# Third and later batches loaded in six pieces instead of four, and 50 dummy matmuls of two widths instead of 30 of one

## The chip, the cores and the metric

One NeuronCore of one Trainium2 chip runs the whole program, attention and expert layer, as one launch. The metric is the device time of one execution in microseconds (us).

## What is computed

Eight batches of eight heads attend over 576 positions of 64 dimensions, each query to itself and the 63 positions before it. The result is laid out as 4608 tokens of 512 numbers. A gate gives each token a score for each of eight experts; all scores are taken in descending order, and a token goes to the expert of its best score that still has room (576 tokens each). Each expert is two matrix products with a ReLU between them.

```python
scores = scale * np.matmul(q, k.transpose(0, 1, 3, 2))
mask = (rel >= 0) & (rel < 64)          # rel = pos_q - pos_k
attn = softmax(np.where(mask, scores, -1e9))
x = (attn @ v)                          # -> (4608, 512)
logits = x @ w_gate                     # -> (4608, 8)
for idx in np.argsort(-logits.flatten()):   # greedy, cap 576 tokens an expert
    ...
out[mask_e] = np.maximum(x[mask_e] @ w1[e], 0.0) @ w2[e]
```

## The kernel before

The program has two stages, one after the other. The first is attention, some 150 us; the second takes the experts one after another.

Attention works on blocks of 64 positions, nine in a batch, and on two blocks at once: iteration `m` of the loop in `attention` (`M` is 36) takes blocks 2m and 2m+1 of the 72. `qk` (L128) multiplies queries by the keys of the block and the one before; VectorE adds the mask and takes the row's extreme (L136); ScalarE takes the exponential (L141); `tr` turns the result on TensorE (L148), ScalarE copies it out (L153); `pv` (L178), two iterations later, multiplies by V; `norm` divides on VectorE (L218, tile `x`) and hands `x` to a list of stores. Once for each batch, `gate_mm` (L85) multiplies a transposed copy of V (tile `VT`) by the gate's weights, `gate_cp`, `gate_tr` and `gate_out` (L89, L95, L101) put the result into spare columns of the V tile `VO`, and GpSimd makes a shifted copy `VE` (L114, L115). For batches 3 to 7 both halves of `gate_mm` stand in the batch's first iteration: eight matmuls for blocks 0 to 3, eight for blocks 4 to 8.

All loads and the stores of `x` are issued by SyncE in the order in which they are written. Batches 0 and 1 are loaded in slices written out by hand (L235 to L253). From the third batch on `load_all` (L255) loads `Q` and `K` (part 0) and, an iteration later, `VT` and `VO` (part 1); each of the four tensors goes in four DMAs (L267), 288 KB or 292 KB each, 2304 or 2336 bytes in each of 128 partitions, and what is left of `VO` in a fifth (L269). In DRAM `lay` has put the data of one DMA together. Stores are held back: `HOLD` is 14, and tile `x` has `HOLD + 4` = 18 buffers, so the `x` of iteration j+18 is written into the buffer that the store of j has read.

Each DMA that SyncE issues takes one of eight completion semaphores in turn, and waits until the DMA that had that semaphore before has landed.

Before anything has arrived, TensorE runs `WARM` dummy matmuls of 128 columns on a tile of zeros (L48, L49); their result is never read.

Of the kernel before, what the change touches and what calls it, by code (L numbers as in the profile page):

```python
# [20 lines left out]
B, H, S, D = 8, 8, 576, 64  # L21
NB = S // 64
HP = H // 2
E = 8
WARM = 30
VW = 73
DM = H * D
HOLD = 14
LOADED = 9 * (B - 3) + 12


def attention(ctx, tc, c, q, k, v, vt, gate, xs, L, choices, setup, counters, mean, rows, guess):

    nc = tc.nc
    wgbd, wg = gate
# [6 lines left out]
    x = ps.tile([128, 512], FT, name="Tp", bufs=2)  # L42
    SP = [ps.tile([128, 2, 4, 128], FT, name=f"Sp{r}", bufs=1) for r in range(2)]

    z = c["zero"]
    nc.vector.memset(z, 0.0)

    for _ in range(WARM):  # L48
        nc.tensor.matmul(x[:, 0:128], z, z, start=True, stop=True)  # L49
    masks(tc, c)  # L50
    Q, K, VO, VE, VT = {}, {}, {}, {}, {}

# [202 lines left out]
    def load_all(b, part):  # L255
        if not part:
            Q[b] = ld.tile([128, NB, HP, 64], FT, name="Q", bufs=3)
            K[b] = ld.tile([128, NB, HP, 64], FT, name="K", bufs=3)
        else:
            VT[b] = ld.tile([128, NB, HP, 64], FT, name="VT")  # L260
            VO[b] = ld.tile([128, 5, H, VW], FT, name="VO", bufs=3)
        for t, x in ((VT[b], vt), (VO[b][:, 0:4], v)) if part else ((Q[b], q), (K[b], k)):
            t = t.rearrange("p i h w -> p (i h w)").rearrange("p (n x) -> p n x", n=4)
            n = 512 * t.shape[2]
            rows = x[b].rearrange("p x -> (p x)")[0:n].rearrange("(n p x) -> n p x", n=4, p=128)
            for i in range(4):
                nc.sync.dma_start(t[:, i], rows[i])  # L267
        if part:
            nc.sync.dma_start(VO[b][0:64, 4].rearrange("p h w -> p (h w)"),  # L269
                              v[b].rearrange("p x -> (p x)")[n:n + 64 * H * VW].rearrange("(p x) -> p x", p=64))  # L270
# [13 lines left out]
    def store(m, x):  # L284
        nc.sync.dma_start(xs[128 * m:128 * m + 128], x.rearrange("p h d -> p (h d)"))
# [5 lines left out]
    for m in range(M + 1):  # L291
# [62 lines left out]
        for s in (2 * m, 2 * m + 1):  # L354
            if stores and (len(stores) > HOLD or s > LOADED):
                store(*stores.pop(0))
        for x in loads.get(m, []):
            load_all(*x)
# [26 lines left out]
def masks(tc, c):  # L385

    nc, cp = tc.nc, c["pool"]
    jp, rel = c["jp"], c["rel"]
    nc.vector.tensor_copy(rel[0:64], jp[0:64])
    nc.vector.tensor_scalar(rel[64:128], jp[64:128], 64, None, op0=OP.add)  # L390
    far = cp.tile([128, 128], FT, name="far")
    near = cp.tile([128, 128], FT, name="near")
    c["mask"] = {}

    def make(kinds):
        m = c["mask"][kinds] = cp.tile([128, 128], FT, name=f"mask{kinds[0]}{kinds[1]}")
        for a, kind in enumerate(kinds):
            r = slice(64 * a, 64 * a + 64)
            if kind:
                nc.vector.tensor_tensor(m[r], far[r], near[r], OP.add)  # L400
            else:
                nc.vector.tensor_scalar(m[r], rel[r], 0.0, -8.0e9, op0=OP.is_gt, op1=OP.mult)

    nc.vector.tensor_scalar(far, rel, 0.0, -8.0e9, op0=OP.is_le, op1=OP.mult)
    nc.vector.tensor_scalar(near, rel, 64.0, -8.0e9, op0=OP.is_gt, op1=OP.mult)
    make((0, 1))
    make((1, 1))
    c["ident"] = cp.tile([128, 128], FT, name="ident")
    c["identr"] = cp.tile([128, 128], FR, name="identr")
    nc.vector.tensor_scalar(c["identr"], jp, 0.0, None, op0=OP.is_equal)  # L410
    nc.vector.tensor_scalar(c["ident"], jp, 0.0, None, op0=OP.is_equal)
    make((1, 0))


def lay(q, k, v, wg):
    import numpy as np
    def blocks(t):
        t = t.reshape(B, HP, 2, NB, 64, D).transpose(0, 2, 5, 3, 1, 4)
        return np.ascontiguousarray(t).reshape(B, 128, NB * HP * 64)

    va = np.zeros((B, 640, H, VW), np.float32)
    va[:, :S, :, :D] = v.transpose(0, 2, 1, 3)
    va[:, :S, :, VW - 1] = 1.0
    va = np.ascontiguousarray(va.reshape(B, 5, 128, H * VW).transpose(0, 2, 1, 3)).reshape(B, 128, 5 * H * VW)

    def pieces(t, n):

        t[2:] = t[2:].reshape(B - 2, 128, n, -1).transpose(0, 2, 1, 3).reshape(B - 2, 128, -1)
        return t

    wb = np.zeros((128, HP, 32), np.float32)
    w = wg.reshape(HP, 2, D, E)
    wb[0:64, :, 0:8] = w[:, 0].transpose(1, 0, 2)
    wb[64:128, :, 16:24] = w[:, 1].transpose(1, 0, 2)
    return dict(q=pieces(blocks(q), 4), k=pieces(blocks(k), 4), v=pieces(va, 5), vt=pieces(blocks(v), 4), wg=wb)


NT = 4608
# [976 lines left out]
def body(tc, q, k, v, vt, wg, w1, w2, xs, out):  # L1415
    nc = tc.nc
    with ExitStack() as ctx:
# [6 lines left out]
        with ExitStack() as actx:  # L1424
            attention(actx, tc, c, q, k, v, vt, (wgs, wg), xs, L, lambda j0, j1: rt.choices(j0, j1, 0), rt.setup,
                      rt.counters, (rt.mean, rt.mean_mm, rt.mean_out), rt.rows, rt.guess)
# [49 lines left out]
```

## Time and profile before

| what | us |
|---|---|
| median of 3 runs (lowest, highest) | 612.87 (612.52, 614.18) |
| the profiled execution: its own time | 613.34 |
| its span, first to last instruction | 611.7 |
| PE busy in the span (5713 matmuls, with as many weight loads) | 588.9 |
| ACT busy | 371.8 |
| DVE busy | 394.1 |

The span lies 1.64 us below the profiled execution's own time. In the profile PE is the matmul unit of TensorE and PEld its weight loads, DVE is VectorE, ACT ScalarE, POOL GpSimd and SP SyncE; L12 is line 12 of the kernel, and `out<-in` names tiles. "issue" as the reason of a wait means that nothing in the profile ended it. Queue q1 holds the DMAs that SyncE issues; the queue of kind "instruction" with the number q8 moves packets of 16 KB.

### The profile page before, as it was taken

The numbers are of one execution on the slowest core, as the hardware profiler recorded it, in microseconds if no ns is written. First come the engines' busy times: TensorE is split into PE (matmuls) and PEld (weight loads), VectorE is DVE, ScalarE is ACT, GpSimd is POOL, SyncE is SP. The second block draws the span as 40 slices with busy tenths as digits, with TensorE's granted clock in tenths as the row PEclk, the third lists the DMA queues.
The fourth block names the chain that finished last, engine by engine and source line by source line (L and its number), as shares of the span: only waits on it lengthen the run. The fifth ranks groups of instructions, "written<-read, shape, count | busy, mean of one in ns | idle before, by whom it ended". The sixth has DMA issues, their size and how long they took to land.

```text
span 611.7 us, 15537 instructions
## 1 busy us (share of the span) xinstructions
PE 588.9 (96%) x5713; PEld 503.3 (82%) x5713; DVE 394.1 (64%) x1804; ACT 371.8 (61%) x804; POOL 198.4 (32%) x277
## 2 busy tenths in 40 slices
PE   7899999997699999999999999999999999999995
PEld 6677878886499789878988997898899789889984
DVE  6798988888785587369547936773685466705400
ACT  6799989997465477267537735852774375615410
POOL 1334435862431261054117203511530273011011
PEclk9999999998699999999999999999999999999999
DMA  8999999962698699189748938992895689410001
GB/s 314 362 359 358 362 365 376 384 240 89 183 242 173 247 210 243 43 289 229 152 167 229 245 70 270 216 221 97 257 243 111 233 191 330 169 44 34 2 26 53
DMA packets 46104, 128.87 MB, mean 211 GB/s; under 512 B 5824, under 2 KB 6464, under 8 KB 46016
## 3 DMA queue, kind: packets, MB, share of 16 engines
q1 hardware_dynamic: 31744, 79.00, 36.0%
q0 software_dynamic: 13984, 48.25, 34.1%
q8 instruction: 46, 0.75, 0.5%
q10 hardware_dynamic: 288, 0.52, 0.3%
q14 instruction: 42, 0.34, 0.2%
HBM read 82.14 MB, written 18.87 MB: 165 GB/s over the span
## 4 chain that ended last, share of the span: by engine, by line
PE 50%; issue 15%; DMA 5%; POOL 2%; DVE 1%; ACT 1%; POOLq 0%; SPq 0%
PE h L1328 23%; PE o L1372 20%; PE o L1362 4%; DMA st<-w 2%; DMA wl<-st 2%; POOL out L1351 2%; PE tp L1266 1%; DMA xg<-xs,idx 1%; PE rps L685 1%; PE rps L1046 1%; POOL xg L1228 0%; ACT wh L1155 0%; POOLq L1472 0%; POOL wl L1171 0%; DVE hl L1297 0%
## 5 line engine op out<-in xcount | busy, mean ns | idle before, releaser
L1328 PE MATMUL h<-xh,wh 128*128 128x320 f32 (+2 forms) x800 | 159.0, 333 | 0.3 <-DVE hh L1297 0.3
L1328 PEld LDWEIGHTS h<-xh,wh 128*128 128x128 f32 x800 | 124.2, 188 | 5.6 <-ACT sum L1287 0.5
L1351 POOL DMA_INDIRECT out<-ot,idx x40 | 40.1, 1001 | 198.1 <-DVE q L932 82.1
L1372 PE MATMUL o<-wh,hl 128*128 128x512 f32 x256 | 101.3, 396 | 0.0
L1372 PE MATMUL o<-wl,hh 128*128 128x512 f32 x256 | 100.5, 393 | 0.0
L1372 PE MATMUL o<-wh,hh 128*128 128x512 f32 x256 | 100.4, 392 | 0.0
L141 ACT ACTIVATE pe<-st,mx 128x128 f32<-128x128 f32 x288 | 92.0, 394 | 5.4 <-DVE mx L136 5.0
L1328 PE MATMUL h<-xh,wl 128*128 128x256 f32 (+1 forms) x512 | 91.1, 298 | 0.0
L1328 PEld LDWEIGHTS h<-xh,wl 128*128 128x128 f32 x512 | 78.5, 188 | 4.1
L1171 POOL DMA_DIRECT2D wl<-st x51 | 45.9, 1023 | 82.1 <-ACT wl L1169 43.8
L1155 ACT ACTIVATE wh<-st 128x1024 fp32r<-128x1024 f32 x64 | 67.3, 1051 | 4.9 <-DMA st<-w 4.7
L1342 ACT ACTIVATE ot<-o 128x512 f32<-128x512 f32 x32 | 19.2, 599 | 83.7 <-PE o L1372 83.7
L136 DVE CUSTOM_DVE_ANT_0 st<-Sp,mask 128x128 f32<-128x128 f32 x288 | 63.7, 285 | 5.9 <-PE Sp L128 4.5
L1372 PEld LDWEIGHTS o<-wl,hh 128*128 128x128 f32 x256 | 48.1, 188 | 9.5
L1372 PEld LDWEIGHTS o<-wh,hh 128*128 128x128 f32 x256 | 48.1, 188 | 9.4
L1372 PEld LDWEIGHTS o<-wh,hl 128*128 128x128 f32 x256 | 48.1, 188 | 9.3
L1169 ACT ACTIVATE wl<-wh 128x1024 fp32r<-128x1024 f32 x51 | 53.9, 1058 | 1.0
L1289 DVE TENSOR_TENSOR sum<-h,sum 128x256 f32<-128x256 f32 x56 | 23.4, 418 | 40.3 <-ACT sum L1287 39.7
L1292 ACT ACTIVATE hh<-h 128x320 fp32r<-128x320 f32 (+1 forms) x72 | 30.8, 427 | 30.2 <-PE h L1328 30.0
L1228 POOL DMA_INDIRECT xg<-xs,idx x32 | 32.4, 1012 | 42.2 <-DVE eq L970 34.6
L1297 DVE SCALAR_TENSOR_TENSOR hl<-h,hh 128x256 fp32r<-128x256 f32 x72 | 30.0, 417 | 24.1 <-ACT hh L1292 24.0
L153 ACT ACTIVATE pt<-Tp 128x512 f32<-128x512 f32 x70 | 41.1, 587 | 6.7 <-PE Tp L148 6.6
(222 smaller groups left out, 1028.4 us busy)
## 6 DMA issues: line engine op xcount, KB each, us to landing
st<-w SPq DMA_DIRECT2D x59, 512.0 KB, 7.6
wl<-st POOLq DMA_DIRECT2D x51, 512.0 KB, 8.6
xs<-x SPq DMA_DIRECT2D x36, 256.0 KB, 5.8
VO<-v SPq DMA_DIRECT2D x24, 292.0 KB, 6.4
Q<-q SPq DMA_DIRECT2D x24, 288.0 KB, 6.9
K<-k SPq DMA_DIRECT2D x24, 288.0 KB, 6.2
VT<-vt SPq DMA_DIRECT2D x24, 288.0 KB, 5.8
st<-w POOLq DMA_DIRECT2D x5, 512.0 KB, 7.9
```

The costliest lines, as they stand in the source:

```text
L136: nc.vector.tensor_tensor_reduce(st[:, h, :], Sp[h % 2][:, h // 2], mk, scale=-0.125, scalar=3.0e38, op0=OP.add, op1=OP.min, accum_out=mx[ ...
L141: nc.scalar.activation(pe[:, h, :], st[:, h, :], AF.Exp, bias=mx[:, h:h + 1], scale=-1.0)
L153: return pt, lambda: nc.scalar.activation(flat, Tp, AF.Copy)
L1155: nc.scalar.activation(hi, st[i], AF.Copy)
L1169: nc.scalar.activation(lo, hi.bitcast(FT), AF.Copy, scale=-1.0)
L1171: nc.gpsimd.dma_start(lo.bitcast(FT), st[i], accum_op=OP.add)
L1228: nc.gpsimd.indirect_dma_start(out=g[a][0:n], out_offset=None, in_=self.xs, in_offset=IndirectOffsetOnAxis(ap=idx[0:n, a:a + 1], axis=0))
L1292: nc.scalar.activation(hh[:, f, c0:c1], h, AF.Relu)
L1297: nc.vector.scalar_tensor_tensor(t, h[:, a - c0:b - c0], 0.0, hh[:, f, a:b].bitcast(FT), op0=OP.max, op1=OP.subtract)
L1328: nc.tensor.matmul(h[:, 0:w], wv[:, cc, 128 * (f % 2):128 * (f % 2) + 128], x[:, cc, x0:x0 + w], start=(k == 0), stop=(k == 4 * len(terms) ...
L1351: nc.gpsimd.indirect_dma_start(out=self.out[5 * p + a], out_offset=IndirectOffsetOnAxis(ap=idx[0:m, a:a + 1], axis=0), in_=ot[0:m], in_off ...
L1372: nc.tensor.matmul(o, ht[:, f, 128 * a:128 * a + 128], wt[:, 512 * (f % 2):512 * (f % 2) + 512], start=(k == 0), stop=(k == 23))
```

## The change

In `load_all` each of the four tensors of a batch from the third on goes in six DMAs of 192 KB (1536 bytes in a partition; for `VO` 1536 or 1664 bytes) in place of four; `pieces` computes the cuts, and `lay` puts the data in DRAM in the new order. The remainder of `VO` and the first two batches are as they were. The 30 dummy matmuls of 128 columns become 32 of 16 columns and then 18 of 128, all with the same 128x128 weights of zeros.

```diff
-WARM = 30
+WARM, SHORT = 18, 32
+def pieces(n):
+    cuts = [n * i // (6 * 32) * 32 for i in range(7)]
+    return list(zip(cuts, cuts[1:]))

-    for _ in range(WARM):
-        nc.tensor.matmul(x[:, 0:128], z, z, start=True, stop=True)
+    for n in [16] * SHORT + [128] * WARM:
+        nc.tensor.matmul(x[:, 0:n], z, z[:, 0:n], start=True, stop=True)

-            t = t.rearrange("p i h w -> p (i h w)").rearrange("p (n x) -> p n x", n=4)
-            n = 512 * t.shape[2]
-            rows = x[b].rearrange("p x -> (p x)")[0:n].rearrange("(n p x) -> n p x", n=4, p=128)
-            for i in range(4):
-                nc.sync.dma_start(t[:, i], rows[i])
+            t = t.rearrange("p i h w -> p (i h w)")
+            rows = x[b].rearrange("p x -> (p x)")
+            n = 128 * t.shape[1]
+            for i, j in pieces(t.shape[1]):
+                nc.sync.dma_start(t[:, i:j], rows[128 * i:128 * j].rearrange("(p x) -> p x", p=128))
```

## Rows read from the trace of the kernel before

**Rows 1.** Busy us by stretch: PE, PEld, DVE, ACT, POOL; clock, DMA share, GB/s.

```profile
20.00:131.00 111.00, 108.71 (x2220) 87.27 (x2217) 97.79 (x679) 102.81 (x307) 56.39 (x105) 1.00 1.03 368
131.00:150.00 19.00, 16.52 (x365) 14.45 (x362) 16.70 (x101) 17.56 (x62) 9.10 (x16) 1.00 0.21 81
```

**Rows 2.** Waits of the weight loads, 0 to 150: total us, times, longest.

```profile
PEld Op L178 <- issue: 5.4, 14, 1.5
...
PEld Tp L85 <- issue: 2.5, 4, 2.0
```

**Rows 3.** Waits of SyncE, 0 to 160: total us, times, longest.

```profile
SPq L267 <- DMA VO<-v: 15.1, 25, 1.8
```

**Rows 4.** Timeline of PE, 14.9 to 22: start, us, what, [idle before].

```profile
15.09 1.10 PE L128 MATMUL Sp<-K,Q 64*64 64x128 f32 x32
...
18.24 0.73 PE L85 MATMUL Tp<-VT,wgs 128*32 128x320 f32 x5 [1.39 <-issue]
...
21.79 0.45 PE L128 MATMUL Sp<-K,Q 64*64 64x128 f32 x8
```

**Rows 5.** Timeline of PEld, 86.3 to 90.

```profile
88.87 0.13 PEld L178 LDWEIGHTS Op<-VE,pt 128*64 128x64 f32 x1 [1.47 <-issue]
```

**Rows 6.** Timeline of all engines, 44 to 66: three successive iterations.

```profile
44.00 1.10 PE L128 MATMUL Sp<-K,Q 64*64 64x128 f32 x32
...
48.20 1.10 PE L128 MATMUL Sp<-K,Q 64*64 64x128 f32 x32
...
51.49 1.10 PE L128 MATMUL Sp<-K,Q 64*64 64x128 f32 x32
```

**Rows 7.** DMA queues: packets, MB, share; the whole span, then 18.24 to 88.87.

```profile
q8 instruction: 46, 0.75, 0.5%
...
q8 instruction: 11, 0.18, 1.1%
```

**Rows 8.** Timeline of SyncE: issues of DMAs, x how many in the row.

```profile
17.33 0.43 SPq L67 DMA_DIRECT2D Q<-q  x1
17.81 0.43 SPq L67 DMA_DIRECT2D K<-k  x1
...
22.67 3.05 SPq L267 DMA_DIRECT2D Q<-q  x4
...
46.14 2.59 SPq L267 DMA_DIRECT2D VT<-vt  x4
...
98.28 2.55 SPq L285 DMA_DIRECT2D xs<-x  x4
```

**Rows 9.** DMA queue q1, 124 to 128 (2048-byte packets), then 25.1 to 28.

```profile
q1 hardware_dynamic: 877, 1.60, 105.0%
...
q1 hardware_dynamic: 292, 1.20, 102.1%
```

**Rows 10.** Issue to landing: VT issued at 48.3, xs at 98.28, xs after 130.

```profile
DMA to landing us min/median/max: 7.4/7.4/7.4
...
DMA to landing us min/median/max: 6.3/6.3/6.3
...
DMA to landing us min/median/max: 2.0/2.0/2.1
```

**Rows 11.** Timeline: gate_mm of batch 3, and the write of x(24).

```profile
57.11 1.18 PE L85 MATMUL Tp<-VT,wgs 128*32 128x256 f32 x16
...
109.14 0.68 DVE L218 TENSOR_TENSOR x<-Op,r 128x512 f32<-128x512 f32 x1
```

**Rows 12.** Lines L49 and L1048: ns min/median/max, first and last start us.

```profile
L49 PE MATMUL Tp<-zero x30: 288/314/315, 1.1 to 4.2; 128*128 128x128 bf16 x30
...
L1048 PE MATMUL rps<-B,R x18: 247/248/270, 158.2 to 159.2; 128*72 128x64 bf16 x18
```

**Rows 13.** Line L128, semaphore instructions of its queue, in the same columns.

```profile
L128 PEldq EVENT_SEMAPHORE  x18: 51/51/51, 4.9 to 123.0; - x18
```

More of the change, by code (lines that the diff above doesn't have):

```diff
@@ L424, in lay, with apart @@
     va = np.ascontiguousarray(va.reshape(B, 5, 128, H * VW).transpose(0, 2, 1, 3)).reshape(B, 128, 5 * H * VW)
-    def pieces(t, n):
-        t[2:] = t[2:].reshape(B - 2, 128, n, -1).transpose(0, 2, 1, 3).reshape(B - 2, 128, -1)
+    def apart(t, n):
+        cuts = pieces(n) + [(n, t.shape[2])] * (n < t.shape[2])
+        t[2:] = np.concatenate([t[2:, :, i:j].reshape(B - 2, -1) for i, j in cuts], 1).reshape(B - 2, 128, -1)
         return t
@@ L434, in lay @@
     wb[64:128, :, 16:24] = w[:, 1].transpose(1, 0, 2)
-    return dict(q=pieces(blocks(q), 4), k=pieces(blocks(k), 4), v=pieces(va, 5), vt=pieces(blocks(v), 4), wg=wb)
+    n = NB * HP * 64
+    return dict(q=apart(blocks(q), n), k=apart(blocks(k), n), v=apart(va, 4 * H * VW), vt=apart(blocks(v), n), wg=wb)
 NT = 4608
```

## The prediction

> **What bounds the kernel now.** I first read the busy time by stretch, because the change touches only the attention stage. From 20 to 131 us PE, ACT and DVE are busy 98, 93 and 88% of the time and the DMA engines 103% by the profile's account, at 368 GB/s [rows 1]. After 131 the DMA share is 0.21 with the compute engines as busy as before [rows 1]: the loads are done some 19 us before attention is. So the DMA queue is full, but it runs ahead of the work, and what sets the end of attention is the chain PE, DVE, ACT, with an iteration of 3.29 us (48.20 to 51.49) and 4.20 us where a half `gate_mm` is added (44.00 to 48.20) [rows 6]. Whatever attention gains or loses goes to the end: the expert stage starts from its last result.
>
> Next I looked in the waits of TensorE's queue for time that this chain doesn't explain. No wait for a load stands among the large ones. Two are put down to "issue", which is nothing that the profile knows: 2.0 us in `gate_mm` and 1.5 us in `pv` [rows 2]. The timeline places them. The iteration that starts at 15.09 ends at 21.79, 6.70 us in place of 4.20, with PE stopped until 18.24 in the middle of eight matmuls on one load, of which three had run; the other stop ends at 88.87, after 1.47 us [rows 4, 5]. I read both as **instruction fetches that come late**. Queue q8 moves 46 packets of 16 KB in the run, against 11,426 matmuls and weight loads, about one for 250 of them, and between the ends of the two stops lie exactly 11 such packets [rows 7]. TensorE's stream is thus read in blocks of some 250 instructions, through the DMA engines that the loads fill, and a block that is still behind loads stops TensorE.
>
> The loads in front of it are many: a load from the third batch on takes 6 to 7 us to land where the engines are busy [rows 10], and SyncE spends its time waiting for the eighth DMA back [rows 3]. At 288 KB that is 2.36 MB in flight.
>
> **Loads in six pieces.** Eight in flight become 1.57 MB, two thirds. What a fetch has to wait behind shrinks in that proportion if it waits behind all of it. The stop at 88.87 lasted 1.47 us, and the other 13 "issue" waits at that line are 0.30 us each ((5.4 - 1.5) / 13) [rows 2], so **1.2 us** are to be had. The bounds are 0 (the fetch waits for something else) and 1.5. I take 1.2, since a third off a wait of several us is more than the stop.
>
> The price is in the packets. Between 124 and 128 us they are of 2048 bytes, with one of 4 bytes for every eight: 877 x 8/9 = 780 took 4 x 16 x 1.050 = 67.2 us, 86.2 ns each. From 25.1 to 28 the mean is 1.20 MB / 260 = 4620 bytes, and 2.9 x 16 x 1.021 / 260 = 182.2 ns [rows 9]. The slope is 0.0373 ns a byte, so a packet of 1536 bytes should take 67.1 ns and one of 2304 95.8; three of the first against two of the second are 201.3 against 191.6, **5.1% more**. From below the price is 0 (the bytes are the same). I take 5.1%, because 2048 is near. Loads from the third batch on begin at 22.67 [rows 8].
>
> [...]
>
> Is there cover for it? I looked for the first places where loads are nearly late. (1) The second eight `gate_mm` of batch 3 start half way through 57.11 to 58.29, at about 57.6 [rows 11]; the last quarter of `VT` that they read, the fourth issue of the row at 46.14, went out at 48.3 and landed 7.4 us later, at 55.7 [rows 8, 10]. Slack 1.9; loss until then (48.3 - 22.7) x 5.1% = 1.3; **left 0.6**. (2) The write of x(24) at 109.14 needs the store of x(6), issued at 98.28 and landed 6.3 later, at 104.6 [rows 8, 10, 11]. Slack 4.5; this store stands behind five whole batches, so the loss is at most (98.28 - 22.67) x 5.1% = 3.9, less for the stores among them, say 3.4; **left 1.1**. Against the times of before nothing is late, but what is left is also the most that compute can run ahead of its old times: 0.6 at batch 3, 1.1 at x(24). At the end the loads finish 4 us later and the last 25 stores, queued behind them on SyncE, catch up 4 us later, inside the stretch that has a DMA share of 0.21: cost 0.
>
> SyncE issues eight DMAs more a batch. Unhindered it issues one in 0.48 us (17.33 to 17.81) [rows 8]; a piece will take the engines 8 x 67.1 = 537 ns. It keeps up, narrowly. Eight pieces in flight are 4.3 us of work, and a store issued alone lands in 2.0 [rows 10], so the engines don't run dry. Each piece is one landing more to wait for: 48 in all. The nearest row is a semaphore instruction of TensorE's queue, 51 ns [rows 13]: 48 x 51 = 2.4 us from above if all are on PE's path, 0 if they pass while TensorE waits for DVE or ACT anyway. I take 0, since the waits of this kind are there now, 18 of them, without an iteration that shows it.
>
> **The dummy matmuls.** 30 start between 1.1 and 4.2, 107 ns apart [rows 12], which is 128 columns at 1.2 GHz, the lower level. Eighteen of them are 1.9 us. For the 32 short ones no row is of that size. With 18 matmuls of 64 columns at the lower level, 60 ns apart (158.2 to 159.2) [rows 12], 32 take 1.9 us from above; from below 16/128 of 107 ns, 0.4 us. Together 2.3 to 3.8 in place of 3.2; the first real matmul waits for its load until 4.9 anyway [rows 13], and 1.1 + 3.8 = 4.9 just reaches it. Cost 0. If weight loads hold them to 107 ns they end at 6.5 and the first matmul comes 1.6 us late. If TensorE came to its upper level later after them, an iteration before 16 us would lose about the 1.10 us that its first 32 matmuls take [rows 4], ahead of a stop that hides it if it stays. What they do beside that: 20 matmuls with their weight loads are **40 instructions more** ahead of everything, so every block of the stream ends 40 instructions earlier in the work. The block whose end stopped PE at 18.24 would end in the matmuls that start at 15.09 [rows 4], and its fetch be asked for about 1 us earlier, behind less. That stop may shrink from 2.0 us to nothing, or stay and only sit elsewhere; the early loads are unchanged. Bounds 0 and 2.0; I take 1.0, of which the 0.6 of place (1) can pass.
>
> [...]
>
> **The sum.** 0.6 at the start and 1.2 at 88 make 1.8, and place (2) lets 1.1 through. From the profiled execution's 613.34: 612.2. It lies 0.47 above the median of 612.87, so against the median 611.8.
>
> **The rivals.** *First case, the forecast*: 611.8, between 611.0 and 612.5. Chance 0.42. *Second, the fetch is late for another reason, or the stops move*: TensorE's blocks end elsewhere and one of the next ends stops it as long. For it: both stops come when a block's crossing and the queue meet by chance, and of the blocks between them none stopped PE long; against it: less is in flight. No gain, 612.9, between 612.5 and 613.7. Chance 0.30. *Third, the pieces cost nothing* (bytes set the rate, the bound of 0): then, if both stops go, place (1) lets 1.9 through and place (2) 4.5, and the gain is 1.9 + 1.2 = 3.1: 609.8. [...] Chance 0.16. *Fourth, SyncE or the packets become the bound and attention waits for loads*: it decides where a DMA takes over 0.55 us, since then the loss at x(24), five batches of 24, passes the 1.1 left. An issue takes 0.48 unhindered and (3.05 - 0.43) / 3 = 0.87 in the row at 22.67, waits for landings included [rows 8]; I price the case a quarter of the way, at 0.58. A batch then takes 24 x (0.58 - 0.537) = 1.0 longer than in the forecast, and x(24) comes 5 x 1.0 - 1.1 = 3.9 late: 612.87 + 3.9 = 616.8. For it: the margin of 0.48 against 0.54 is thin; against it: 0.48 was reached with the queue full. Late dummies or 2.4 us of semaphores would end near it, at 614.5 to 615.3. Chance 0.12.
>
> **How the numbers follow.** About 0.3%, 1.8 us, is what a measurement of this kernel can tell from no change: below 611.0 is faster, above 614.7 slower. The third case (0.16) and a quarter of the first, where the packets cost half of what I take (0.10), make 0.26 faster; the fourth, without its mildest part, makes 0.10 slower; 0.64 lies within. The range goes from the third case's 609.8 to 614.2, which leaves most of the fourth and the tail of the third outside, some 2 in 10.
>
> **What would show it.** Right: the wait of 1.47 us before `pv` is gone and no other "issue" wait over 1 us stands after 23 us; the stop near 16 us is shorter; DMA rates of 350 to 365 GB/s from 23 to 115; x(24) is written right after the store of x(6) lands. Wrong: PE waiting for `VT`, `K` or `VO` (fourth case), the first real matmul after 5.0 (dummies), a DMA rate as before (third), or stops of the same length at other lines (second).

## The result and the profile after

The changed kernel takes 620.17 us (median of five runs, 619.59 to 622.30) against 612.87 us: **slower by 7.3 us**, ratio 1.0123 with a 95% interval of 1.0098 to 1.0148. The profiled execution took 621.69, its span is 620.0. The forecast was 611.8, at most 614.2; what came lies beyond even the fourth case.

The loss is all in attention. Its last `qk` starts at 148.2 in the profiled execution and at 139.4 in that of before, 8.8 us later; from there to the end both take the same within 0.5 us. The rows, of the kernel before and of the changed one:

```profile
139.43 1.10 PE L128 MATMUL Sp<-K,Q 64*64 64x128 f32 x32
```

```profile
148.25 1.10 PE L134 MATMUL Sp<-K,Q 64*64 64x128 f32 x32
```

The same stretches as [rows 1], busy us by engine, clock, DMA share and GB/s:

```profile
20.00:131.00 111.00, 101.85 (x2032) 82.05 (x2031) 88.94 (x616) 92.86 (x275) 51.13 (x93) 0.97 0.97 318
131.00:150.00 19.00, 19.00 (x407) 15.60 (x405) 17.39 (x120) 18.07 (x55) 13.07 (x27) 1.00 0.93 344
```

The loads now come at 318 GB/s in place of 368, and they go on behind 131 us, where the DMA share was 0.21 and is 0.93. The share between 20 and 131 has hardly fallen (1.03 to 0.97), so the share alone would not have told. The time of a packet counts in full, however slow it is: from 23 to 115 us the changed kernel's packets of 1536 bytes take 65 ns in the median, 75.7 in the mean and up to 1.7 us. The rate tells.

The waits up to 150 us (total, times, longest) name the places:

```profile
PEld Op L184 <- issue: 4.6, 14, 0.7
...
PEld Tp L91 <- issue: 3.9, 3, 3.4
...
DVE x L224 <- DMA xs<-x: 3.4, 1, 3.4
PE Tp L91 <- DMA VT<-vt: 3.0, 1, 3.0
...
DVE VO L107 <- DMA VO<-v: 1.7, 1, 1.7
```

L184 is `pv`: its longest "issue" wait is 0.7 us where [rows 2] had 1.5. L91 is `gate_mm`: its "issue" wait of 3.4 us is no late fetch but the weight load beside the 3.0 us in which TensorE waits for `VT`. The timeline of TensorE shows both sides of the trade, the stop of [rows 4] gone and the iteration of place (1) drawn out:

```profile
15.38 1.10 PE L134 MATMUL Sp<-K,Q 64*64 64x128 f32 x32
...
19.98 0.83 PE L134 MATMUL Sp<-K,Q 64*64 64x128 f32 x16
...
56.05 1.10 PE L134 MATMUL Sp<-K,Q 64*64 64x128 f32 x32
57.97 0.64 PE L91 MATMUL Tp<-VT,wgs 128*32 128x256 f32 x8 [0.81 <-ACT pe L147]
61.58 0.92 PE L91 MATMUL Tp<-VT,wgs 128*32 128x320 f32 x8 [2.97 <-DMA VT<-vt]
...
65.99 0.56 PE L134 MATMUL Sp<-K,Q 64*64 64x128 f32 x12
```

The iteration at 15.38 takes 4.60 us, 2.1 less than in [rows 4]. The one at 56.05 takes 9.94, where the same one of before takes 4.34:

```profile
56.08 1.10 PE L128 MATMUL Sp<-K,Q 64*64 64x128 f32 x32
...
60.42 1.10 PE L128 MATMUL Sp<-K,Q 64*64 64x128 f32 x32
```

The waits of 0.81 and 2.97 us are 3.8 of the 5.6 us that it lost. Most of the rest is a second price of the stop. After it the granted clock of TensorE (the third number from the right) is below 1.00:

```profile
61.58:66.00 4.42, 4.42 (x49) 3.41 (x50) 1.25 (x6) 1.29 (x4) 0.46 (x1) 0.61 0.86 259
```

The mean of 0.61 is 3.4 us, from 62.0 to 65.4, at 0.50, the lower of the two levels, 1.00 and 0.50, that its records show. From the second eight `gate_mm` to the next `qk` it now takes 4.41 us, where before it took some 2.8 (57.6, half way through that row of [rows 11], to 60.42). The clock falls to 0.50 a second time, from 120.0 to 123.5, behind the stop at place (2). In the kernel before it stays at 1.00 between 20 and 131 us. Place (2) shows in VectorE's timeline (compare [rows 11]):

```profile
117.80 0.69 DVE L224 TENSOR_TENSOR x<-Op,r 128x512 f32<-128x512 f32 x1 [3.37 <-DMA xs<-x]
```

Two more views tell how the loads are fed. SyncE's waits up to 160 us, the first line of them beside [rows 3]:

```profile
SPq L273 <- DMA VO<-v: 5.0, 9, 1.6
SPq L273 <- DMA K<-k: 5.0, 10, 1.1
SPq L273 <- DMA VT<-vt: 4.4, 11, 2.2
SPq L273 <- DMA Q<-q: 3.7, 9, 1.6
```

By these lines SyncE waited 39 times for a landing for 144 loads, 18.1 us in all; the first line of before alone has 25 waits and 15.1 us for 96 loads. So SyncE was more often behind the engines than before. Even so, counted from issue to landing over 23 to 115 us, 7.6 DMAs were in flight on average, and 7.95 before: most of the time there were nearly eight. Part 6 of the page gives KB and median us from issue to landing, first of the kernel before, then of the changed one:

```profile
VO<-v SPq DMA_DIRECT2D x24, 292.0 KB, 6.4
Q<-q SPq DMA_DIRECT2D x24, 288.0 KB, 6.9
K<-k SPq DMA_DIRECT2D x24, 288.0 KB, 6.2
VT<-vt SPq DMA_DIRECT2D x24, 288.0 KB, 5.8
```

```profile
Q<-q SPq DMA_DIRECT2D x36, 192.0 KB, 4.4
K<-k SPq DMA_DIRECT2D x36, 192.0 KB, 4.5
VT<-vt SPq DMA_DIRECT2D x36, 192.0 KB, 5.3
VO<-v SPq DMA_DIRECT2D x30, 192.0 KB, 4.8
```

A piece is two thirds of the old size but takes 0.64 to 0.91 of the old time to land. Eight in flight that land 4.4 to 5.3 us after their issue are 8 x 196.6 KB / 4.4 to 5.3 = 357 to 297 GB/s, and 318 lies between. This is a balance and names no cause: in the kernel before, 8 x 294.9 KB in 5.8 to 6.9 us are 407 to 342 GB/s, and 368 lies between too. What it shows is that the way from issue to landing shrank less than the bytes in flight. The timeline of SyncE shows what happens when one issue is slow:

```profile
74.12 2.02 SPq L273 DMA_DIRECT2D VO<-v  x4
...
76.70 2.60 SPq L291 DMA_DIRECT2D xs<-x  x1
79.40 2.79 SPq L273 DMA_DIRECT2D Q<-q  x6
82.23 2.39 SPq L273 DMA_DIRECT2D K<-k  x3
```

The store at 76.70 held SyncE for 2.60 us. In that time the engines work off more than half of what eight pieces are, and SyncE, at about 0.47 us an issue behind it (2.79 / 6), is slow to refill them against their need of about 0.54 (the prediction's estimate, 8 x 67.1 ns). In the trace a packet of 16 KB on q8, the queue of kind "instruction", is under way from 76.5 to 78.9, nearly as long as that issue. The DMA view from 76.4 to 79 us has it:

```profile
q8 instruction: 1, 0.02, 5.9%
```

The last section comes back to this.

### The profile page after: what moved, and what is told of

It reads as the page before. It is cut to its first block, busy times and chain, and to the rows that moved or that the text cites. A ratio compares the mean times of both kernels' runs of the same rounds, so it can differ in the third digit from the quotient of the medians.

```text
span 620.0 us, 15652 instructions
## 1 busy us (share of the span) xinstructions
PE 591.4 (95%) x5733; PEld 506.2 (82%) x5733; DVE 393.9 (64%) x1804; ACT 372.5 (60%) x804; POOL 198.4 (32%) x277
## 4 chain that ended last, share of the span: by engine, by line
PE 52%; issue 14%; DMA 3%; POOL 2%; ACT 1%; POOLq 0%; SPq 0%
PE h L1336 25%; PE o L1380 21%; PE o L1370 4%; DMA wl<-st 2%; POOL out L1359 1%; PE tp L1274 1%; PE rps L693 1%; DMA st<-w 1%; PE rps L1054 1%; ACT wh L1163 0%; ACT wl L1177 0%; POOL xg L1236 0%; POOLq L1480 0%; POOL wl L1179 0%; ACT xh L1224 0%
## 5 line engine op out<-in xcount | busy, mean ns | idle before, releaser
L1236 POOL DMA_INDIRECT xg<-xs,idx x32 | 32.4, 1011 | 42.2 <-DVE eq L978 34.6
```

The costliest lines, as they stand in the source:

```text
L1236: nc.gpsimd.indirect_dma_start(out=g[a][0:n], out_offset=None, in_=self.xs, in_offset=IndirectOffsetOnAxis(ap=idx[0:n, a:a + 1], axis=0))
```

## The experiments

Four theories. **A**: 1.57 MB in flight is too little. **B**: packets of 1536 bytes are slow. **C**: SyncE, with half as many DMAs again, becomes the bound. **D**: the dummies move TensorE's fetches and delay the early loads. Each ratio is to the kernel before on the same chip. The rate is that from 20 to 131 us of the profiled execution. Where the loads end earlier than 131 (at 120 to 130 us in the kernel before, e1, e3, e4, e6, e10, e11 and e12), it is held down by that, so the table at the end of this section also has the rate from 68 to 115 us, in which all kernels load.

**Dummies alone** (`e1_dummies_alone`).

```diff
-    cuts = [n * i // (6 * 32) * 32 for i in range(7)]
+    cuts = [n * i // 4 for i in range(5)]
```

> The dummies of the change, with loads in four DMAs of 288 KB. The changed kernel lost 7.3 us, and shows its first load from the third batch on landing 2.3 us later than the kernel before, since a fetch for TensorE came at 10.7 in place of 15.6 us. If the loads are the cause (theory A: too few bytes in flight; theory B: packets of 1536 bytes; theory C: 48 more issues of SyncE), this kernel is at 610 to 613 us, a little under the kernel before if the stop of 2.0 us near 16 us is gone and nothing stops later. If the dummies are the cause (theory D: the shifted fetches delay the early loads and everything after them), it is at 618 or more.

613.41 us, ratio 1.0008 (0.9985 to 1.0030).

```profile
20.00:131.00 111.00, 108.29 (x2214) 86.84 (x2214) 96.88 (x675) 101.31 (x301) 55.31 (x104) 1.00 1.03 370
```

Rate and time are those of before: D falls. In its profile the stop near 16 us is gone too (the iteration takes 4.59 us), but three "issue" waits of 0.5 us or more follow, the longest of 0.9 us, and attention's last `qk` starts at 139.0 where it was 139.4: of 2.1 us won 0.4 is left. What the dummies give at one place they take at others.

**Six pieces alone** (`e2_six_alone`), with the 30 old dummies.

```diff
-WARM, SHORT = 18, 32
+WARM, SHORT = 30, 0
```

> Six pieces with the 30 dummies of before. Theories A, B and C: 618 to 622 us, with waits for VT of batch 3 and for the store of x(6) again, and loads that end near 133 us. Theory D: 612 to 613. In between, at 615 to 617, the six pieces alone are not enough, and the 2.3 us that the early loads lose by the shifted fetch carry a part.

619.70 us, ratio 1.0109 (1.0084 to 1.0133), at 324 GB/s. The pieces carry the whole loss. Of the waits, the store of x(6) is the larger here:

```profile
DVE x L224 <- DMA xs<-x: 7.0, 2, 5.6
...
PE Tp L91 <- DMA VT<-vt: 2.0, 3, 1.2
```

**The same packets, more in flight** (`e3_three_of_two_packets`).

```diff
 ...
-            for i, j in pieces(t.shape[1]):
-                nc.sync.dma_start(t[:, i:j], rows[128 * i:128 * j].rearrange("(p x) -> p x", p=128))
+            cuts = pieces(t.shape[1])
+            for (i, _), (_, j) in zip(cuts[::2], cuts[1::2]):
+                nc.sync.dma_start(t[:, i:j].rearrange("p (n x) -> p n x", n=2),
+                                  rows[128 * i:128 * j].rearrange("(n p x) -> p n x", n=2, p=128))
```

> The dummies of the change; each tensor in three DMAs of 384 KB, with two packets of 1536 (for VO also 1600) bytes in a partition: the packets of the six pieces, but eight DMAs are 3.1 MB in flight in place of 1.57, and SyncE issues 24 fewer a batch pair. Theory A (bytes in flight) and theory C (issues): no loss, 610 to 613 us, loads done at 121 to 125. Theory B (the packets): as slow as the changed kernel, 618 to 622, loads done near 135.

616.30 us, ratio 1.0060 (1.0038 to 1.0081).

```profile
20.00:131.00 111.00, 106.07 (x2149) 85.20 (x2147) 93.97 (x653) 97.93 (x291) 55.42 (x104) 0.98 1.05 364
```

Packets of 1536 bytes reach 364 GB/s, and neither `VT` nor a store is waited for: B falls as the cause. But no theory had expected 616. The waits tell why:

```profile
PEld Op L185 <- issue: 6.7, 15, 2.1
...
PEld Tp L155 <- issue: 1.2, 1, 1.2
```

With 3.1 MB in flight TensorE stops again, for 2.1 us and for 1.2. That these stops are late fetches, as the prediction read those of before, fits the trace: they end at 43.47 and 78.63, 1.2 and 1.5 us after a packet of q8 has landed (42.2, 77.1). In the kernel before it was 1.3 and 1.5 us (16.9 and 87.4, to 18.24 and 88.87), and in its trace 2815 matmuls, weight loads and semaphore instructions of TensorE lie between the ends of the two, 256 for each of the 11 packets of [rows 7]; between two "issue" waits of the changed kernel, 0.83 us to 36.45 and 0.74 us to 80.26, lie 1536 and 6 packets, 256 again. Behind the longer stop of e3 the clock stands at half from 43.4 to 46.8.

**Long packets** (`e4_three_pieces`): three DMAs of 384 KB with one packet of 3072 bytes in a partition.

```diff
-    cuts = [n * i // (6 * 32) * 32 for i in range(7)]
+    cuts = [n * i // (3 * 32) * 32 for i in range(4)]
```

> The dummies of the change; each tensor in three DMAs of 384 KB with one packet of 3072 bytes in a partition. Theories A, B and C all say that the loads end earlier than with four DMAs, at 118 to 121 us. If the fetches for TensorE wait behind all that is in flight, as the prediction held, the stops grow and this is slower than the kernel with four DMAs and the same dummies by 1 to 3 us; if they don't, it is the same within 0.5 us or faster.

617.19 us (613.48 to 618.87; the profile is of the fastest), ratio 1.0082 (1.0058 to 1.0106), at 367 GB/s, the longest "issue" wait 1.4 us. From 23 to 115 us, while both load, the means are 362 GB/s in e3 and 375 here:

```profile
DMA packets 21182, 33.29 MB, mean 362 GB/s; under 512 B 1430, under 2 KB 18763, under 8 KB 21158
```

Packets of twice the length, 3072 bytes against 1536 with the same bytes in flight, win 4% in rate here and no time.

**Few in flight, few issues** (`e9_four_in_flight`): the kernel e3, in which each load waits besides for the fourth load before it.

```diff
+    flying = []
 ...
+                if len(flying) > 3:
+                    tc.add_manual_dep(ld4.ins, flying[-4].name,
+                                      mybir.DependencyInfo(mybir.DependencyClass.Sync, mybir.DependencyReason.DATA),
+                                      reason="at most four in flight")
+                flying.append(ld4.ins)
```

> Three DMAs of 384 KB a tensor with two packets of 1536 bytes in a partition, each waiting besides for the fourth load before it: 1.57 MB in flight and packets of 1536 bytes as in the changed kernel, but half as many issues of SyncE. Theory A (1.57 MB is too little to have in flight): as slow as the changed kernel, 618 us or more, at 315 to 330 GB/s, loads done at 130 or later. Theory C (SyncE's issues, of 0.49 us each on average in the changed kernel, are the bound, since 87 of 136 of them did not wait for a landing): 350 GB/s or more, loads done by 125, no wait for VT or for a store, 611 to 616.

617.21 us (616.33 to 621.12), ratio 1.0079 (1.0043 to 1.0115).

```profile
20.00:131.00 111.00, 103.81 (x2071) 83.74 (x2067) 90.55 (x634) 94.98 (x281) 53.25 (x98) 0.97 0.99 326
131.00:150.00 19.00, 18.65 (x390) 15.16 (x390) 16.93 (x112) 17.95 (x55) 11.30 (x22) 1.00 0.84 313
```

```profile
DVE x L225 <- DMA xs<-x: 6.2, 2, 4.7
...
PE Tp L92 <- DMA VT<-vt: 1.1, 1, 1.1
```

The time is 0.8 us under what A had asked for, but the rate, the end of the loads behind 131 us and the waits are those of the changed kernel, with half its issues: **A is enough for the slow loads**. The longest "issue" wait is 0.6 us, not 2.1. Against e3 the one edit has turned late fetches into late loads, at nearly the same time.

**Many issues added** (`e13_four_and_small`): e9 with a DMA of 1 KB behind each load.

```diff
 ...
+                nc.sync.dma_start(scrap[16 * (n % 8):16 * (n % 8) + 16, 16 * (n // 8):16 * (n // 8) + 16], q[0, 0:16, 0:16])
```

> Four loads of 384 KB in flight, and behind each a small DMA of 1 KB that goes to a tile nobody reads: SyncE's issues are as many as in the changed kernel, the bytes in flight and the rate of the engines as with four in flight alone. If SyncE's issues add to the loss (theory C beside A), this is 2 to 4 us slower than the 617.2 of that kernel, with a rate of 300 to 318 GB/s; if only the bytes in flight count, it is within 1.5 us of it, at 320 to 330.

623.67 us, ratio 1.0152 (1.0127 to 1.0176), which lies above that of e9 without overlap.

```profile
20.00:131.00 111.00, 102.53 (x2039) 82.19 (x2039) 89.40 (x618) 93.40 (x276) 51.53 (x93) 0.97 0.96 314
```

326 GB/s become 314, the 318 of the changed kernel nearly: at these bytes in flight **more issues add to A**. How much is rough. By the middle values it is 0.7%, some 4.5 us, but the two kernels ran on different chips, each against the kernel before; and by the profiles attention's last `qk` starts 1.9 us later than in e9 (148.0, 146.1), while another 2.3 us lie behind attention, where the edit changes nothing. A rival is left, too: a small DMA takes one of the eight semaphores besides SyncE's time, so while a store is under way fewer than four loads can be. No run separates the two.

**More in flight again** (`e11_six_of_three`): e9 with six in place of four.

```diff
-                if len(flying) > 3:
-                    tc.add_manual_dep(ld4.ins, flying[-4].name,
+                if len(flying) > 5:
+                    tc.add_manual_dep(ld4.ins, flying[-6].name,
```

> The kernel with four loads of 384 KB in flight, with six instead: 2.36 MB, as before the change, again packets of 1536 bytes and half as many issues. Theory A: the rate from 68 to 115 us returns from 325 GB/s to 360 or more, loads done by 125, no wait for VT or a store, and stops by late fetches between those with eight of these in flight (4.9 us) and those with four (1.1): 612 to 615. If something other than the bytes in flight slowed the kernel with four, the rate stays under 340 and the time over 616.

617.89 us, ratio 1.0082 (1.0053 to 1.0110): not the 612 to 615 expected.

```profile
20.00:131.00 111.00, 107.30 (x2192) 86.06 (x2193) 95.68 (x661) 100.16 (x297) 55.71 (x104) 1.00 1.05 362
```

The rate is back and no `VT` or store is waited for, as A has it. The longest "issue" wait, read as a late fetch, is 1.4 us, more than the 0.9 of e1 with 2.36 MB in DMAs of 288 KB, and attention's last `qk` starts at 140.4, 1.0 us after that of before. But the profiled span is 3.0 us longer; the other 2.0 lie behind attention. From the last `qk` to the end the 14 profiles take 471.2 to 474.8 us, though no edit touches that part, so times that differ by 3 us don't rank two kernels by their loads. By time alone e3, e9 and e11 are alike (616 to 618 us at 3.1, 1.57 and 2.36 MB); what sets e9 apart is its rate, its waits and its last `qk`, at 146.1.

**Place (1) relieved** (`e8_place_one`).

```diff
-            m1 = m0 + 1 + 2 * n if b < 3 else m0
+            m1 = m0 + 1 + 2 * n if b < 4 else m0
-            turns.setdefault(m1 + (b > 2), []).append((b, *i))
+            turns.setdefault(m1 + (b > 3), []).append((b, *i))
```

> The changed kernel with the gate's matmuls of batch 3 one and three iterations later, as batches 0 to 2 have them: they no longer need the last piece of VT at 57 us. The wait there and what follows it lengthened the iteration from 4.3 to 9.9 us. If each late load costs by itself (the prediction's places), this is 5 us faster than the changed kernel: 614 to 615. If the loads as a whole are the bound, the time comes back at the store of x(6) or at batch 7: 618 to 621, with attention's last qk at 146 to 149 us as in the changed kernel.

620.09 us, ratio 1.0098 (1.0060 to 1.0136), attention's last `qk` at 148.3.

```profile
DVE x L224 <- DMA xs<-x: 4.9, 2, 3.3
...
DVE VO L107 <- DMA Q<-q: 2.5, 1, 2.5
```

`VT` is not waited for, and nothing is won: the stores are waited for instead, for 4.9 us. (A stop of 2.4 us at `pv` near 102 us is in this profile too, and the clock is at half twice.) So the places don't each have a price; the loads as a whole are the bound, and whoever needs one first pays.

**Other sizes.** Five pieces (`e6_five_pieces`), four with six in flight (`e10_six_in_flight`), the same with place (1) relieved (`e12_six_and_place_one`), and six of half the height (`e5_six_half_height`).

```diff
 # e6
+    cuts = [n * i // (5 * 16) * 16 for i in range(6)]
 ...
 # e10: four pieces, and
+                if len(flying) > 5:
+                    tc.add_manual_dep(ld6.ins, flying[-6].name,
 ...
 # e12: e10, and
+            m1 = m0 + 1 + 2 * n if b < 4 else m0
 ...
 # e5: three pieces, each in two DMAs
+                for h in range(0, 128, 64):
+                    nc.sync.dma_start(t[h:h + 64, i:j], rows[128 * i + (j - i) * h:128 * i + (j - i) * (h + 64)]
+                                      .rearrange("(p x) -> p x", p=64))
```

> Five pieces of 230 KB a tensor with the dummies of the change: 1.84 MB in flight, packets of 1792 to 1856 bytes. Theory A: the rate lies between the 312 GB/s of six pieces and the 375 of four, at 335 to 360 from 68 to 115 us, and the time between 613.4 and 620.2: 614 to 617. A price per packet alone (5.1% for six pieces, about half of it for five) gives 612 to 613.5.

> Four DMAs of 288 KB a tensor and the dummies of the change, each load waiting besides for the sixth load before it: 1.73 MB in flight, near the 1.57 of the changed kernel, with SyncE's issues as before the change. Theory C: full rate, 355 to 368 GB/s, and if less in flight brings TensorE's fetches earlier, as the prediction held, the stops over 0.3 us (1.9 us in all with four DMAs and the same dummies) fall under 1 us: 611 to 613. Theory A: 340 GB/s or less, 614 to 619.

> Four DMAs of 288 KB a tensor with six in flight, and the gate's matmuls of batch 3 one and three iterations later. In the profiled run without the second edit, place (1) cost 4.3 us, at a rate of 326 GB/s until 68 us and 344 after it. If that wait is the only price of six in flight, and the earlier fetches its gain, this takes 609 to 611.5, less than either kernel; if the later matmuls lengthen two iterations for nothing, or the loads come late at another place, 612 to 615.

> Six DMAs of 192 KB a tensor, each of 64 partitions with one packet of 3072 bytes, so bytes in flight and issues are those of the changed kernel and the packets are twice as long and half as many. Theories A and C: as slow as the changed kernel or slower (an issue for 64 partitions took 0.47 us where one for 128 took 0.33), 618 to 624. Theory B (packets of 1536 bytes): 611 to 615.

e6: 613.33 us, ratio 1.0001 (0.9979 to 1.0023). e10: 612.62, ratio 0.9987 (0.9968 to 1.0005). e12: 614.56, ratio 1.0004 (0.9992 to 1.0016). None beats the kernel before. The lines are of e6, of e10 (whose profile is of the slowest of its ten executions, 617.1, where place (1) cost it 4.3) and of e12:

```profile
20.00:131.00 111.00, 108.85 (x2235) 87.43 (x2232) 98.03 (x681) 101.79 (x304) 56.40 (x106) 1.00 1.02 355
```

```profile
20.00:131.00 111.00, 106.42 (x2153) 84.88 (x2151) 94.22 (x653) 98.65 (x294) 55.75 (x104) 0.98 0.99 340
```

```profile
20.00:131.00 111.00, 107.50 (x2194) 85.96 (x2192) 96.34 (x669) 100.69 (x299) 55.39 (x104) 1.00 1.00 355
```

e6 has the rate that A expected but loses nothing by it: 1.89 MB in flight (eight of 236 KB) just do, with 1.3 us of waiting for a store and for `VT`. e12's rows have no wait for `VT` or a store, and it is still not faster, so the wait at place (1) was not what kept e10 from a gain. In the profiles attention's last `qk` starts 1.7 us earlier than before in e6 and 0.3 later in e12; what is won there does not reach the times. For e10 and e12 the bytes in flight are 6 x 294.9 KB = 1.77 MB, not the 1.73 of the expectation. Half height is another matter, and stands in the last section.

The runs side by side, with the start of attention's last `qk` in the profiled execution; in these runs the price of too little in flight sets in between 1.57 and 1.77 MB:

| kernel | MB in flight | DMAs a tensor | GB/s 20 to 131 | GB/s 68 to 115 | last `qk` | ratio |
|---|---|---|---|---|---|---|
| e3, two packets | 3.1 | 3 | 364 | 368 | 142.8 | 1.0060 |
| e4, long packets | 3.1 | 3 | 367 | 382 | 140.4 | 1.0082 |
| before | 2.36 | 4 | 368 | 372 | 139.4 | 1 |
| e1, dummies | 2.36 | 4 | 370 | 375 | 139.0 | 1.0008 |
| e11 | 2.36 | 3 | 362 | 369 | 140.4 | 1.0082 |
| e6, five | 1.89 | 5 | 355 | 349 | 137.7 | 1.0001 |
| e10 | 1.77 | 4 | 340 | 344 | 142.7 | 0.9987 |
| e12, place (1) | 1.77 | 4 | 355 | 358 | 139.7 | 1.0004 |
| e9 | 1.57 | 3 | 326 | 325 | 146.1 | 1.0079 |
| e2, six alone | 1.57 | 6 | 324 | 321 | 146.9 | 1.0109 |
| changed kernel | 1.57 | 6 | 318 | 312 | 148.2 | 1.0123 |
| e8, place (1) | 1.57 | 6 | 313 | 312 | 148.3 | 1.0098 |
| e13 | 1.57 | 3 + 3 small | 314 | 320 | 148.0 | 1.0152 |
| e5, half height | 1.57 | 6 | 280 | 277 | 162.4 | 1.0396 |

## Why the prediction was wrong

**The step that failed** is the one that kept the engines fed: "Eight pieces in flight are 4.3 us of work, and a store issued alone lands in 2.0, so the engines don't run dry", with "it keeps up, narrowly" beside it. It set 4.3 us against the landing of one DMA on an empty queue. In the loaded queue the pieces land 4.4 to 5.3 us after their issue, longer than the 4.3 that eight of them were to last, and no issue may come late; but issues come late, one takes 2.6 us. e9 shows that fewer bytes in flight alone bring the rate down to 326 GB/s, e13 that more issues add to it. Why the way to landing does not shrink as the bytes do is not shown. A piece took 196.6 KB / 318 GB/s = 0.62 us, not 0.537, and that is past the 0.55 at which the prediction let its fourth case begin.

**The fourth case** had the right sign, TensorE waiting for `VT`, and half of the cause, with too small a price and chance: SyncE's issues were in it, but that eight pieces are too few to have in flight was in none of the four. Priced at 0.58 it gave 616.8; with 0.62 its own sum gives 5 x 24 x (0.62 - 0.537) - 1.1 = 8.9, so 621.8 against 620.2 measured. The margin of 0.48 against 0.54 was seen and called thin, and still got 0.12.

**The packets** were sized well. In an undisturbed stretch of the changed kernel, 84.8 to 86.4 us, queue q1 has

```profile
q1 hardware_dynamic: 432, 0.59, 103.1%
```

432 x 8/9 = 384 packets in 1.6 x 16 x 1.031 = 26.4 us, 68.7 ns each, where 67.1 were forecast. e3 shows that this term by itself costs no wait for a load. The landings more to wait for were put at 0, 2.4 us from above; e6 has 24 of the 48, and its time is that of before.

**The gain** came at its places and not in the time. The stop near 16 us gave back 2.1 us (forecast 1.0, bound 2.0), and no "issue" wait of TensorE over 1 us but the one beside `VT` is left after 23. But e1, which has the first part without the pieces, is no faster than before. That less in flight brings the fetches earlier fits most runs: longest "issue" waits (those beside a late load left out) of 2.1 and 1.4 us with 3.1 MB in flight, 0.9 with 2.36 (e1), 0.6 and 0.5 with 1.57 (e9, e2). It is not a rule: e11 has 1.4 with 2.36, e13 has 1.3 with 1.57, and the changed kernel new stops of 0.7 and 0.8. By these rows a fetch behind a full DMA queue (share 1.05 in e3) stopped TensorE for up to 2.1 us.

**Places (1) and (2)** were the places where it broke, named in advance, with the cover taken as 0.6 and 1.1 us. They took 5.6 us (9.94 - 4.34) and 3.4 us of waiting, and the clock fell behind each, for which the prediction had no term: some 1.6 us of the 5.6. But e8 shows that they were symptoms: a rate 14% lower finds another place.

**The end of the loads** was to cost nothing with the loads done 4 us later. They end 15 us later, at 136 us, and with the stores behind them they fill the stretch from 131 to 150 (share 0.93).

**The dummies** cost nothing, as forecast (e1), and the first real matmul starts at 5.0. That the 30 of before ran at the lower level was the author's estimate from 107 ns for 128 columns, 1.2 columns a ns: the clock records of that kernel begin at 6.47 us. It fits its matmuls of 288 columns (L656), which start 240 ns apart at a granted clock of 0.50, 1.2 columns a ns, and 123 ns apart at 1.00. The 32 short ones start 27 ns apart. The early loads were not unchanged, as the prediction had it: the first one from `load_all` lands at 34.1 us in place of 31.9, and at 32.9 in e1, where this costs no time.

**Open**: how the loss of the changed kernel splits between A and C beyond the rough sizes above, and by what mechanism a single issue of SyncE comes to last 1 to 2.6 us (the last section has what goes with it).

## What to carry to other kernels

With a fixed number of DMAs in flight (eight here), cutting each smaller cuts the bytes in flight. Multiply them out, and don't set the time that they last against the landing time of an empty queue: here 2.0 us looked safe against 4.3, the pieces took 4.4 to 5.3, and the rate fell by 14% (368 to 318 GB/s). A kernel that limits the DMAs in flight by a dependency, as e9, tells what fewer bytes cost before anything else is changed. Count the issues of the engine that issues as well, with the longest that the trace shows (2.60 us here): at 0.48 us an issue against 0.54 us of work for the DMA engines there is little left to catch up with. Judge a DMA queue by its rate, since its busy share fell only from 1.03 to 0.97. And price a stop of TensorE with what the clock costs behind it: here 3.4 us at half behind each of two stops.

## What the runs showed of the hardware

**DMAs into 64 partitions were slower here for the same bytes.** e5 moves the same bytes as the changed kernel with the same count of DMAs and twice the packet length, each DMA into 64 partitions, and takes 637.08 us, ratio 1.0396 (1.0365 to 1.0427). All theories had it at 624 at most. The DMA view from 23 to 115 us, of e4 (3072 bytes into 128 partitions) and of e5 (3072 bytes into 64):

```profile
DMA packets 12945, 34.52 MB, mean 375 GB/s; under 512 B 1476, under 2 KB 1476, under 8 KB 12921
...
q1 hardware_dynamic: 12921, 34.21, 101.5%
```

```profile
DMA packets 10065, 25.17 MB, mean 274 GB/s; under 512 B 1890, under 2 KB 1890, under 8 KB 10045
...
q1 hardware_dynamic: 10045, 24.91, 100.4%
```

The engines are full in both, but for a megabyte they take 92 x 16 x 1.015 / 34.21 = 43.7 us in e4 and 92 x 16 x 1.004 / 24.91 = 59.3 in e5, some 36% more. e4 has twice the bytes in flight, but that is not the reason: a packet of 3072 bytes takes 187 ns in the median in e5 and 122 in e4, while one of 1536 takes 65 or 66 at 1.57 MB in flight (changed kernel, e9) as at 3.1 (e3). Why a packet takes longer into 64 partitions no run shows.

**Long issues of SyncE fall together with packets of the instruction queue.** In the traces of all 14 kernels 96 issues between 22 and 131 us last over 1 us (10 in the changed kernel, 4 before). A 16 KB packet of q8 is under way during 95 of them, and during 187 of the 1669 issues under 0.6 us, though q8 is busy only 15 to 18% of that time. Which of the two makes the other slow no run shows.

**A stop of TensorE can cost a second time.** In the changed kernel the granted clock stood at half (0.50) for 3.4 us behind each of the stops of 2.97 and 1.70 us, and in e9 for 6.9 us (114.5 to 121.4) around a stop of 3.07. In the kernel before, e1, e4, e6, e11 and e12 it stayed at 1.00 from 20 to 131 us.

**Late fetches and late loads trade off here.** From 1.57 MB in flight (e9: longest "issue" wait 0.6 us, stores waited for 6.2) to 3.1 (e3: 2.1 us, neither `VT` nor a store waited for) the kernel goes, with exceptions, from late loads to late fetches, and the least time lies flat between 1.77 and 2.4 MB in the table above, where no run differs from the kernel before by more than can be measured, but for e11.
